# An attention and expert kernel on one core: first expert's weight splits behind its chunks, last chunks in block order, new order tables

## The chip, the cores and the metric

One core of a Trainium2 chip runs the whole program. The metric is device time in microseconds (us); lower is better. The engines are TensorE (PE in the profile; its weight loads are PEld), VectorE (DVE), ScalarE (ACT), GpSimd (POOL) and SyncE (SP), which only issues DMAs. ScalarE and GpSimd issue some DMAs of their own.

## The reference

Two layers, float32, 8 batches of 576 tokens. First an attention with landmarks (Nystrom), 8 heads of 64; then a mixture of 8 experts in which a token mostly keeps the expert of the token before it.

```python
# attention, for each batch and head; means over groups of 18 tokens give 32 landmarks
A, Bm, C = sm(q, k_lm), sm(q_lm, k_lm), sm(q_lm, k)
Z = Bm.T / (norm1(Bm) * norminf(Bm) + 1e-6)
for _ in range(6): Z = 2 * Z - Z @ Bm @ Z
x = A @ Z @ C @ v
# experts, for each token s of a batch
fresh = argmax(x[s] @ w_gate)
e = fresh if s == 0 or sigmoid(x[s] @ w_local) < 0.5 else prev_e
out[s] = softmax(x[s] @ w_gate)[e] * (relu(x[s] @ w1[e]) @ w2[e])   # w1 512x1024, w2 1024x512
```

## The kernel before, in words

**Attention.** For each batch the queries and keys come in transposed. `landmarks` (L228) sums groups of 18 tokens on VectorE, after a first halving on GpSimd (L241, L242) except for the first loads (L235, L237), and ScalarE scales them (L247, L249). `scores_c` (L262) is the matmul of landmarks against all keys (L274); `newton_step` (L427) is one step of the inverse (L432 on TensorE, L435 on VectorE), `c_v` (L335) multiplies by the values, `newton_w` (L444) leaves a small matrix `wt` for each head. The attention output is never formed: `w_w1` (L674) multiplies `wt` into the expert's w1 (L694) and splits the product into a high and a low part, `gh` (L707) and `gl` (L708), so that matmuls of the fast float32 kind keep their accuracy. The softmaxed scores are split in the same way (L516 and L520; L528 and L530 in the first batch).

**Experts.** Nearly all tokens of a batch go to one expert. `expert` (L756) runs 16 chunks for each batch: two passes over the tokens (blocks 2, 3, 4 and then 0, 1, of 128 tokens each; block 4 has 64) of 8 chunks f each. A chunk is `mm1` (L728): 6 matmuls (L737), a relu on ScalarE (L746, L748), its low part on VectorE (L749, L752); and, two chunks later (LAG = 2), `after`: three matmuls per full block (L789) and two for block 4 (L781) against chunk f of w2, which is itself split by `split_w2` (L718): ScalarE copies `raw` to `wh` (L720), GpSimd subtracts to give `wl` (L725). At the last chunk of a pass `store` (L800) scales each block and sends it out: ScalarE multiplies (L815) and issues the DMA (L816); block 4 takes L821 to L825. In the last batch block 0 is scaled on VectorE (L805) and sent from SyncE (L806), and block 1 by halves on ScalarE (L810) and VectorE (L811), sent from ScalarE (L812) and SyncE (L813). Between batches 6 and 7 a half-length expert serves up to 128 tokens that left their batch's expert.

**Order of the work.** The program is built with a scheduler: the place in the source is an instruction's priority on its engine, and the scheduler follows a simulated timeline of its own and takes the next ready instruction. The order on each engine is then fixed in the program. The source order comes from a loop over chunks (L1374 on); `events` holds the attention steps of the next batches with a time in chunks (FIRST, SECOND, PLANS, SLOT_AT), and `run` emits those that are due. G_AT, W2_AT place `w_w1` and w2 loads.

**The opening** (`first_attention`, L1013) is emitted by hand, and `line_up` (L198) fixes the order of TensorE, ScalarE, VectorE and GpSimd as emitted. `keep_warm` (L171) issues idle matmuls on zeros, SUMS[i] of them between Newton steps. The first batch's expert is not known from votes as in the others but guessed early: `guess_sums` (L532, matmuls L539), `guess_copy`, `guess_scores` (L547, 8 matmuls L551, a copy L554), `guess` (L556, VectorE L559 and L560), which puts the expert's number into `regs`. `first_weights` (L1221) then lets SyncE read it and issue the loads of w1 (two pieces, L671), of w2 chunks 0 and 1 (L715), of the keys of batch 1, of w1's second half, of w2 chunks 2 and 3 and then 4 to 7. After the opening the source has `cut_w2(0, f)` for f = 0 to 3, then the chunks; at chunk i `cuts_at` adds the split of chunk 4 + i ahead of that chunk's own matmuls. The first 9 chunks' matmuls are fixed in order by `line_up`, while attention steps that `run` emits on the whole chunk are only placed behind what was lined up.

```python
    first_attention(sts[0], sts[1])
    line_up()
    for f in range(4):
        cut_w2(0, f)
    ...
            cuts_at(b, i)      # b == 0: cut_w2(0, 4 + i)
            next(gen)          # mm1 of chunk i, with its relu
            ...
            run(t0 + i + 0.5)
            next(gen)          # after(i - 2)
```

Of the kernel before, what the change touches and what calls it, by code (L numbers as in the profile page):

```python
# [9 lines left out]
F32 = mybir.dt.float32  # L10
# [10 lines left out]
P = 128  # L21
# [55 lines left out]
def nystrom_attn_then_sticky_moe(ctx, tc, qT, kT, v, wg, w12, out):  # L77
# [678 lines left out]
    def expert(st, w2, passes, store, apart=False):  # L756

        waiting = []
        for s0, n, blocks in passes:
            yps, hs = {}, {}  # L760
            for f in range(NC2):
                hs[f] = mm1(st, f, s0, n, apart)
                yield
                if len(waiting) == LAG:
                    waiting.pop(0)()

                def after(f=f, blocks=blocks, yps=yps, hs=hs):
                    full = [k for k in blocks if k < 4]
                    for k in full:
                        if k not in yps:  # L770
                            yps[k] = py.tile([P, DM], F32, name="py")
                    wh, wl = w2[f]
                    h = hs[f][0]
                    if 4 in blocks:


                        for ff in range(0 if f == NC2 - 1 else NC2, NC2) if apart else (f,):
                            if 4 not in yps:
                                yps[4] = pg.tile([P, DM], F32, name="pg")
                            for w in w2[ff]:  # L780
                                nc.tensor.matmul(yps[4], hs[ff][1], w, start=(ff == 0 and w is w2[ff][0]),  # L781
                                                 stop=(ff == NC2 - 1 and w is w2[ff][1]))
                        if f == NC2 - 1:
                            store(4, yps[4])
                    terms = ((0, wh), (0, wl), (384, wh))
                    each = [(i, t) for i in range(len(full)) for t in terms] if f == NC2 - 1 else [
                        (i, t) for t in terms for i in range(len(full))]
                    for i, (part, w) in each:
                        nc.tensor.matmul(yps[full[i]], h[:, part + i * P:part + i * P + P], w,  # L789
                                         start=(f == 0 and part == 0 and w is wh), stop=(f == NC2 - 1 and part == 384))  # L790
                    if f == NC2 - 1:
                        for k in full:
                            store(k, yps[k])

                waiting.append(after)
                yield
        for after in waiting:
            after()

    def store(b, st, k, yp):  # L800
        ys = fk.tile([P, DM], F32, name="ys", bufs=2)
        t0 = b * S + k * P
        if b == B - 1 and k == 0:
# [209 lines left out]
    def first_attention(st, st1):  # L1013
# [288 lines left out]
    SECOND = dict(v=4.1, q0=0.1, k0=0.1, c0=0.6, q2=0.6, k2=1.1, c1=2.6, norms=2.6, a0=6.1, nf=7.1, a1=7.1, t0=7.1,
        amax=8.1, n0=7.6, t2=7.6, n1=7.6, t4=7.6, aexp=8.1, n2=7.6, cv=8.1, n3=7.6, n4=8.1, anorm=8.1, n5=8.1, nw=8.1,
        gw=8.1, aback=8.6, gates=8.6, nwt=11.1, votes=8.6, split=8.6, w1=9.1, w1b=11.2, fresh=11.6, sticky=12.1,
        chosen=14.6, own=17.6)
    STEPS = ("load v q0 k0 c0 q2 k2 c1 norms a0 nf a1 t0 n0 t2 amax n1 t4 aexp n2 cv n3 anorm n4 aback n5 "
             "nw gw gates nwt votes split w1 fresh sticky chosen own").split()
    PLANS = {
        2: (-13.4, -11.4, -9.9, -12.4, -7.9, -9.4, -7.9, -7.4, -6.9, -6.4, -6.9, -4.9, -2.4, -5.4, -1.4, -1.4, 0.1,
            -0.4, -0.9, -0.4, -0.4, 1.1, 2.6, -0.9, 4.6, 4.6, 5.1, 5.6, 7.1, 7.1, 8.1, 10.1, 8.1, 8.1, 8.6, 13.6,  # L1310
            14.1),
        3: (-22.4, -16.9, -19.4, -13.9, None, -15.4, -13.4, -13.4, -13.4, -9.9, -8.4, -8.4, -6.4, -6.9, -2.9, -7.9,
            -8.4, -6.4, -7.9, -4.4, -2.9, -3.9, -3.4, -2.4, 1.1, 2.6, 2.6, 2.6, 3.1, 5.1, 4.1, 4.1, 7.6, 5.1, 7.1,
            11.1, 11.6),
        4: (-24.4, -20.9, -18.4, -17.4, None, -16.4, -15.4, -15.4, -14.9, -14.9, -14.9, -13.4, -11.4, -11.9, -10.9,
            -8.9, -7.4, -7.4, -6.4, -8.4, -6.4, -6.4, -6.4, -7.4, -5.9, -5.4, -3.9, -3.9, 2.6, 4.1, 2.6, 2.6, 3.6,
            4.1, 5.1, 6.6, 11.6),
        5: (-26.9, -20.4, -25.4, -24.4, None, -16.9, -18.4, -16.9, -16.9, -16.4, -12.9, -14.9, -10.9, -11.4, -10.4,
            -11.9, -10.9, -10.4, -7.9, -11.4, -7.9, -9.9, -7.9, -4.4, -3.9, -1.9, -1.4, 0.6, 1.1, 4.1, 2.6, 5.6, 3.6,
            3.6, 4.1, 4.1, 6.6),  # L1320
        6: (-21.4, -17.9, -20.9, -20.4, None, -17.4, -17.9, -16.9, -13.9, -14.9, -13.9, -14.4, -11.4, -13.4, -9.9,
            -12.4, -9.9, -9.9, -5.9, -8.4, -6.9, -9.4, -5.4, -4.9, -0.9, -3.4, -2.9, -2.4, 0.6, 2.6, 1.6, 3.6, 3.1,
            3.1, 3.6, 6.6, 7.6),
        7: (-27.4, -20.4, -25.9, -19.4, None, -20.4, -20.4, -17.4, -14.9, -16.4, -14.9, -13.9, -13.4, -14.4, -11.9,
            -12.9, -11.4, -10.9, -11.9, -10.4, -9.9, -10.4, -10.4, -9.4, -5.4, -6.9, -5.9, -5.4, -0.4, -3.9, -0.4,
            1.1, 1.6, 3.6, 7.6, 7.6, 10.1),
    }
# [40 lines left out]
    first_attention(sts[0], sts[1])  # L1368
    line_up()
    others_ = (ET.Activation, ET.DVE, ET.Pool)  # L1370
    for f in range(4):
        cut_w2(0, f)
    t0 = 0
    for b in SEQ:  # L1374
# [5 lines left out]
        for i in range(LEN[b]):  # L1380
# [64 lines left out]
```

## Time and profile before

| | us |
|---|---|
| three runs | 477.02, 477.85, 478.03; median 477.85 |
| the profiled execution | 476.7 |
| its span, first to last instruction | 474.9 |
| TensorE busy in the span | 456.8 (96%), clock granted 0.994 of full on the mean |
| VectorE, GpSimd, ScalarE busy | 268.7, 231.5, 204.6 |

The profile comes from one execution. Its rows give for a group of instructions the line, the engine, the operation, output and input tiles and shapes, how long they took, and in square brackets how long the engine stood idle before and what ended that. In the table of stretches each row gives a window, its length, and the busy time of each engine with its count of instructions, then the granted TensorE clock (1.00 is 2.4 GHz, 0.50 is 1.2 GHz), the mean busy share of the DMA engines and their GB/s. A DMA row ends with the median time from issue to landing. Matmuls overlap, so that a row of six lasts less than six times one.

### The profile page before, as it was taken

How to read it: one execution, taken by the hardware profiler on the slowest of the kernel's cores; microseconds unless marked ns; L12 is line 12 of the kernel's file. 1: busy time of each engine (PE TensorE's matmuls, PEld its weight loads, DVE VectorE, ACT ScalarE, POOL GpSimd, SP SyncE). 2: the span in 40 equal slices, each digit the busy share in tenths (PEclk: the TensorE clock that was granted, in tenths of full speed). 3: DMA queues.
4: the chain of work that ended last, by engine and by line, in shares of the span. 5: the costliest groups of instructions: out<-in, count | busy, mean ns of one | idle time of the engine just before them, and what ended most of it. 6: DMA issues, size and time to landing. Idle time of an engine off the chain costs nothing.

```text
span 474.9 us, 12149 instructions
## 1 busy us (share of the span) xinstructions
PE 456.8 (96%) x4710; PEld 338.1 (71%) x4710; DVE 268.7 (57%) x824; ACT 204.6 (43%) x518; POOL 231.5 (49%) x365
## 2 busy tenths in 40 slices
PE   8979999999999999999999999999999999999995
PEld 2636667687786777768885687767886887778884
DVE  6887766776477548648633673248549834323211
ACT  2456244554164616355244634354334513555131
POOL 7178473395187508538612542144336755467010
PEclk9989999999999999999999999999999999999999
DMA  8996083964099226937842245523511731762011
GB/s 296 307 382 216 15 307 109 372 229 147 13 359 348 93 67 252 363 93 248 312 153 54 92 158 191 147 73 140 222 58 52 235 130 47 235 218 71 0 57 47
DMA packets 38861, 82.01 MB, mean 173 GB/s; under 512 B 3291, under 2 KB 4827, under 8 KB 38032
## 3 DMA queue, kind: packets, MB, share of 16 engines
q1 hardware_dynamic: 32208, 67.09, 41.2%
q10 hardware_dynamic: 5104, 9.05, 5.4%
q0 software_dynamic: 1488, 5.07, 2.8%
q8 instruction: 38, 0.62, 0.6%
q14 instruction: 23, 0.19, 0.1%
HBM read 66.29 MB, written 14.94 MB: 171 GB/s over the span
## 4 chain that ended last, share of the span: by engine, by line
PE 76%; DVE 7%; DMA 6%; issue 4%; ACT 3%; POOL 2%; SPq 1%; ACTq 0%; POOLq 0%; DVEq 0%
PE py L789 33%; PE ph L737 20%; PE pg L781 5%; DMA raw<-w 3%; PE ph L694 3%; PE one L432 2%; PE one L345 2%; DMA k_t<-kT 2%; PE one L482 2%; PE one L331 2%; DMA q_t<-qT 1%; PE one L304 1%; PE one L274 1%; DVE h L749 1%; POOL t L241 1%
## 5 line engine op out<-in xcount | busy, mean ns | idle before, releaser
L789 PE MATMUL py<-wh,h 128*128 128x512 f32 x528 | 170.4, 402 | 1.4 <-ACT ys L815 1.1
L725 POOL TENSOR_TENSOR wl<-raw,wh 128x512 fp32r<-128x512 f32 x68 | 86.9, 1294 | 73.2 <-ACT wh L720 65.0
L789 PEld LDWEIGHTS py<-wh,h 128*128 128x128 f32 x528 | 95.1, 188 | 29.2 <-issue 7.1
L746 ACT ACTIVATE h<-ph 128x256 fp32r<-128x256 f32 (+2 forms) x136 | 54.7, 403 | 128.9 <-PE ph L737 115.1
L749 DVE SCALAR_TENSOR_TENSOR h<-ph,h 128x256 fp32r<-128x256 f32 (+1 forms) x136 | 55.6, 410 | 94.0 <-ACT h L746 88.7
L789 PE MATMUL py<-wl,h 128*128 128x512 f32 x264 | 91.4, 393 | 0.0
L737 PE MATMUL ph<-ath,gh 128*128 128x320 f32 (+1 forms) x256 | 79.9, 312 | 1.9 <-DVE h L749 1.0
L737 PE MATMUL ph<-atl,gh 128*128 128x320 f32 (+1 forms) x256 | 75.8, 296 | 0.4 <-DVE atl L530 0.4
L737 PE MATMUL ph<-ath,gl 128*128 128x320 f32 (+1 forms) x256 | 75.8, 296 | 0.0
L737 PEld LDWEIGHTS ph<-ath,gh 128*128 128x128 f32 x256 | 48.1, 188 | 17.4 <-issue 6.2
L789 PEld LDWEIGHTS py<-wl,h 128*128 128x128 f32 x264 | 49.5, 188 | 10.8 <-issue 0.8
L737 PEld LDWEIGHTS ph<-atl,gh 128*128 128x128 f32 x256 | 48.1, 188 | 4.0 <-DVE atl L530 0.7
L737 PEld LDWEIGHTS ph<-ath,gl 128*128 128x128 f32 x256 | 48.2, 188 | 0.9 <-issue 0.7
L720 ACT CAST wh<-raw 128x512 fp32r<-128x512 f32 x68 | 41.0, 631 | 15.7 <-DMA raw<-w 13.9
L824 POOL TENSOR_TENSOR ys<-ys,yl 64x512 f32<-64x512 f32 x8 | 10.2, 1276 | 40.1 <-ACT yl L822 40.1
L494 POOL TENSOR_TENSOR sa<-sa,mxa 128x1152 f32<-128x1152 f32 x7 | 14.9, 2131 | 21.8 <-DVE mxa L493 21.8
L815 ACT ACTIVATE ys<-py,pall 128x512 f32<-128x512 f32 x30 | 19.9, 692 | 11.4 <-DMA out<-ys 8.3
L241 POOL TENSOR_TENSOR t<-q_t 128x288 f32<-128x288 f32 x28 | 21.4, 785 | 4.3 <-DVE sk L242 1.7
L708 DVE TENSOR_TENSOR gl<-ph,gh 128x512 fp32r<-128x512 f32 (+1 forms) x19 | 12.4, 656 | 18.7 <-ACT gh L707 18.7
L781 PE MATMUL pg<-wl,h 128*128 128x512 f32 x56 | 22.4, 400 | 0.0
L781 PE MATMUL pg<-wh,h 128*128 128x512 f32 x56 | 22.3, 399 | 0.0
L707 ACT CAST gh<-ph 128x512 fp32r<-128x512 f32 (+1 forms) x19 | 10.6, 564 | 25.2 <-PE pg L694 24.3
(338 smaller groups left out, 729.2 us busy)
## 6 DMA issues: line engine op xcount, KB each, us to landing
raw<-w SPq DMA_DIRECT2D x68, 256.0 KB, 5.3
raw<-w SPq DMA_DIRECT2D x17, 1024.0 KB, 6.9
v_t<-v SPq DMA_DIRECT2D x8, 1024.0 KB, 6.0
out<-ys ACTq DMA_DIRECT2D x30, 256.0 KB, 2.6
q_t<-qT SPq DMA_DIRECT2D x6, 1152.0 KB, 5.7
k_t<-kT SPq DMA_DIRECT2D x6, 1152.0 KB, 8.7
ad<-sa POOLq DMA_DIRECT2D x8, 576.0 KB, 3.1
q_t<-qT SPq DMA_DIRECT2D x4, 576.0 KB, 9.3
```

Of the source, the lines that this page charges most:

```text
L241: nc.gpsimd.tensor_add(t9[:, i], src[:, a + i, :, 0:9], src[:, a + i, :, 9:18])
L494: nc.gpsimd.tensor_tensor(out=sa, in0=sa, in1=mx.unsqueeze(2).broadcast_to([P, 2 * NJ, M]), op=ALU.subtract)
L694: mm = nc.tensor.matmul(ps[g][32 * c:32 * c + 32, 0:n * P], w, w1[r, n * i:n * i + n, a * P:a * P + P], start=True, stop=True)
L708: last = nc.vector.tensor_tensor(out=gl[:, g, x], in0=ps[g][:, 0:n * P], in1=gh[:, g, x].bitcast(F32), op=ALU.subtract)
L720: cut = nc.scalar.copy(out=wh, in_=raw)
L725: nc.gpsimd.tensor_tensor(out=wl, in0=raw, in1=wh.bitcast(F32), op=ALU.subtract)
L737: mm = nc.tensor.matmul(hp, w[:, g, c], x[:, g, s0:s0 + n], start=(i == 0), stop=(i == 5))
L746: nc.scalar.activation(out=h[:, 0:e], in_=hp[:, 0:e], func=AF.Relu)
L749: nc.vector.scalar_tensor_tensor(out=h[:, 384:384 + m], in0=hp[:, 0:m], scalar=0.0, in1=h[:, 0:m].bitcast(F32), op0=ALU.max, op1=ALU.subtract)
L781: nc.tensor.matmul(yps[4], hs[ff][1], w, start=(ff == 0 and w is w2[ff][0]), stop=(ff == NC2 - 1 and w is w2[ff][1]))
L789: nc.tensor.matmul(yps[full[i]], h[:, part + i * P:part + i * P + P], w, start=(f == 0 and part == 0 and w is wh), stop=(f == NC2 - 1 and ...
L815: nc.scalar.mul(out=ys, in_=yp, mul=st["pw"][:, k:k + 1])
```

## The change

Six edits. (1) In `first_attention` the matmuls that guess the expert go ahead of two idle matmuls, and the VectorE part of the guess goes ahead of the second half of the score maxima, `c_exp(1)` and Newton step 1; SUMS[0] goes from 2 to 1. (2) Only w2 splits 0 and 1 are emitted ahead of the first chunk; split 2 + i is emitted behind `mm1` of chunk i. (3) In the last chunk of every pass the matmuls on w2 are chained in the order written: three for one block, then three for the next. (4) In the last batch block 0 is scaled on ScalarE as other blocks are, block 1 on VectorE in one piece, and both are sent from ScalarE's queue. (5) SECOND, FIRST, PLANS, G_AT, SLOT_AT, W2_AT have new numbers. (6) `cuts_at` no longer splits for batch 0.

```diff
                     terms = ((0, wh), (0, wl), (384, wh))
                     each = [(i, t) for i in range(len(full)) for t in terms] if f == NC2 - 1 else [
                         (i, t) for t in terms for i in range(len(full))]
+                    mms = []
                     for i, (part, w) in each:
-                        nc.tensor.matmul(yps[full[i]], ...)
+                        mms.append(nc.tensor.matmul(yps[full[i]], ...))
+                    if f == NC2 - 1:
+                        in_row(mms)
...
-        if b == B - 1 and k == 0:
+        if b == B - 1 and k == 1:
             nc.vector.tensor_scalar(out=ys, in0=yp, scalar1=st["pw"][:, k:k + 1], scalar2=None, op0=ALU.mult)
-            nc.sync.dma_start(out=out[t0:t0 + P, :], in_=ys)
-        elif b == B - 1 and k == 1:
-            yr = fk.tile([P, 256], F32, name="yl", bufs=1)
-            nc.scalar.mul(out=ys[:, 0:256], in_=yp[:, 0:256], mul=st["pw"][:, k:k + 1])
-            nc.vector.tensor_scalar(out=yr, in0=yp[:, 256:512], scalar1=st["pw"][:, k:k + 1], scalar2=None, op0=ALU.mult)
-            nc.scalar.dma_start(out=out[t0:t0 + P, 0:256], in_=ys[:, 0:256])
-            nc.sync.dma_start(out=out[t0:t0 + P, 256:512], in_=yr)
+            nc.scalar.dma_start(out=out[t0:t0 + P, :], in_=ys)
         elif k < 4:
             nc.scalar.mul(out=ys, in_=yp, mul=st["pw"][:, k:k + 1])
             nc.scalar.dma_start(out=out[t0:t0 + P, :], in_=ys)
...
-        SUMS = (2, 2, 2, 2)
+        SUMS = (1, 2, 2, 2)
...
         newton_step(0, st, 0)
         idle = psa.tile([P, 512], F32, name="one")
+        guess_scores(st)
         keep_warm(SUMS[1], idle)
-        guess_scores(st)
+        guess(st)
         c_max(1, 1)
         c_exp(1)
         newton_step(0, st, 1)
-        guess(st)
         keep_warm(SUMS[2], idle)
...
     def cuts_at(b, i):
-        if i < 5:
+        if b and i < 5:
             cut_w2(b, NC2 - 5 + i)
-        if b == 0 and i < 4:
-            cut_w2(b, NC2 - 4 + i)
...
-    SECOND = dict(v=4.1, q0=0.1, k0=0.1, c0=0.6, q2=0.6, k2=1.1, c1=2.6, ..., split=8.6, w1=9.1, w1b=11.2, fresh=11.6, ...
+    SECOND = dict(v=3.6, q0=0.1, k0=0.6, c0=0.6, q2=0.1, k2=1.1, c1=1.6, ..., split=10.1, w1=8.6, w1b=9.7, fresh=10.1, ...
-    FIRST = dict(rs=0.6, rm=0.6, re=0.6, rn=1.1, rb=2.1, gw=3.1, gates=3.6, votes=5.6, fresh=6.1, ...
+    FIRST = dict(rs=0.1, rm=0.1, re=0.1, rn=1.6, rb=2.6, gw=1.6, gates=3.6, votes=5.1, fresh=5.6, ...
-    W2_AT = (11, 12, 12, 12, 12, 15)
+    W2_AT = (10, 12, 12, 13, 15, 15)
...
-    for f in range(4):
+    for f in range(2):
         cut_w2(0, f)
...
             cuts_at(b, i)
             next(gen)
+            if b == 0 and i < NC2 - 2:
+                cut_w2(b, 2 + i)
             if t0 + i < IN_ROW:
                 line_up((ET.PE,), others_ if i < 4 else ())
```

In PLANS (batches 2 to 7, 37 steps each) 70 entries move earlier, 68 later, and the rest stay; most by half a chunk or one, the farthest by 3.5 chunks (`split` of batch 2, later) and 3 (`w1` of batch 7, later). G_AT of batch 4 goes from chunks (11, 14) to (10, 13); SLOT_AT moves by 0.5 to 2.5 chunks.

## Rows read from the trace of the kernel before

**Rows 1.** The page's head: span, and busy time of TensorE and its weight loads.
```profile
span 474.9 us, 12149 instructions
PE 456.8 (96%) x4710; PEld 338.1 (71%) x4710; DVE 268.7 (57%) x824; ACT 204.6 (43%) x518; POOL 231.5 (49%) x365
```

**Rows 2.** Table of stretches: window, length, busy us by engine, clock, DMA share, GB/s.
```profile
30.00:32.70 2.70, 0.17 (x2) 0.00 (x0) 2.09 (x5) 1.79 (x6) 1.41 (x2) 1.00 1.08 394
32.70:36.10 3.40, 3.36 (x32) 0.93 (x32) 2.54 (x9) 1.74 (x7) 3.40 (x5) 0.50 1.00 407
36.10:42.00 5.90, 5.90 (x46) 4.00 (x44) 3.48 (x8) 4.87 (x16) 5.90 (x6) 1.00 0.35 129
42.00:54.00 12.00, 10.92 (x83) 8.30 (x79) 11.14 (x45) 5.11 (x20) 8.32 (x17) 1.00 0.45 147
54.00:469.20 415.20, 409.52 (x4149) 311.50 (x4149) 225.33 (x695) 179.31 (x434) 197.02 (x275) 1.00 0.47 162
469.20:474.90 5.70, 0.00 (x0) 0.00 (x0) 1.01 (x2) 0.47 (x1) 0.00 (x0) 0.84 0.27 95
```

**Rows 3.** The chain of waits, 20 to 33 us: start, us, what.
```profile
23.23 8.27 DMA raw<-w
```

**Rows 4.** Timeline, 27 to 33 us, ScalarE, VectorE and TensorE: start, length, instruction.
```profile
27.02 1.15 ACT L720 CAST wh<-raw 128x512 fp32r<-128x512 f32 x2
28.02 0.74 DVE L242 TENSOR_REDUCE sq<-t 128x64 f32<-128x576 f32 x1
...
30.85 1.29 ACT L720 CAST wh<-raw 128x512 fp32r<-128x512 f32 x2 [2.68 <-DMA raw<-w]
...
32.05 0.38 ACT L746 ACTIVATE h<-ph 128x256 fp32r<-128x256 f32 x1
...
32.43 0.26 ACT L247 ACTIVATE ql<-sq 128x64 f32<-128x64 f32 x1
...
32.74 1.94 PE L274 MATMUL one<-k_t,ql 64*32 64x288 f32 x12 [2.57 <-ACT ql L247]
```

**Rows 5.** Timeline, 16 to 19 us: the guess of the expert and the Newton update beside it.
```profile
16.27 0.60 PE L176 MATMUL one<-zeros 128*128 128x512 bf16 x2
...
16.71 0.45 DVE L1052 TENSOR_REDUCE mx<-ph 128x1 f32<-128x288 f32 x1
...
17.10 0.17 ACT L554 COPY tot<-one 128x8 f32<-128x8 f32 x1 [0.91 <-PE one L551]
...
17.55 0.29 DVE L435 TENSOR_TENSOR et<-ph,et 128x128 f32<-128x128 f32 x1 [0.20 <-PE ph L432]
...
18.03 0.16 DVE L560 FIND_INDEX8 regs<-top,tot 128x8 uint32<-128x8 f32 x1
...
18.93 0.99 SPq L671 DMA_DIRECT2D raw<-w  x2
```

**Rows 6.** TensorE's waits over the whole span: us in total, times, longest.
```profile
PE py L789 <- ACT ys L815: 1.1, 2, 0.6
```

**Rows 7.** Timeline of the tail: last matmuls, VectorE's scaling, SyncE's last store.
```profile
468.56 0.61 PE L789 MATMUL py<-wh,h 128*128 128x512 f32 x2
469.05 0.75 DVE L805 TENSOR_SCALAR ys<-py,pall 128x512 f32<-128x512 f32 x1 [2.18 <-PE py L789]
...
470.28 0.37 SPq L813 DMA_DIRECT2D out<-yl  x1
```

**Rows 8.** DMA issues by line: count, KB each, median us to landing.
```profile
raw<-w SPq DMA_DIRECT2D x68, 256.0 KB, 5.3
...
out<-ys ACTq DMA_DIRECT2D x30, 256.0 KB, 2.6
...
out<-yl SPq DMA_DIRECT2D x1, 128.0 KB, 2.6
```

**Rows 9.** VectorE's L520 by length (min/median/max ns), and the wait behind the longest.
```profile
L520 DVE TENSOR_TENSOR atl<-at,ath x7: 1324/1357/2737, 82.3 to 378.2; 128x1152 fp32r<-128x1152 f32 x7
...
190.33 0.39 PE L737 MATMUL ph<-ath,gh 128*128 128x256 f32 x1 [0.99 <-DVE h L749]
```

More of the change, by code (lines that the diff above doesn't have):

```diff
@@ L787, in after @@
                         (i, t) for t in terms for i in range(len(full))]
+                    mms = []
                     for i, (part, w) in each:
-                        nc.tensor.matmul(yps[full[i]], h[:, part + i * P:part + i * P + P], w,
-                                         start=(f == 0 and part == 0 and w is wh), stop=(f == NC2 - 1 and part == 384))
+                        mms.append(nc.tensor.matmul(yps[full[i]], h[:, part + i * P:part + i * P + P], w,
+                                                    start=(f == 0 and part == 0 and w is wh), stop=(f == NC2 - 1 and part == 384)))
+                    if f == NC2 - 1:
+                        in_row(mms)
                     if f == NC2 - 1:
@@ L1300, in at_time @@
         events.append((t, len(events), fn))
[L1302 to L1305, printed above, removed]
+    SECOND = dict(v=3.6, q0=0.1, k0=0.6, c0=0.6, q2=0.1, k2=1.1, c1=1.6, norms=2.6, a0=6.1, nf=7.1, a1=7.1, t0=7.6,
+        amax=7.6, n0=7.6, t2=7.6, n1=7.6, t4=7.6, aexp=8.1, n2=7.6, cv=7.6, n3=7.6, n4=8.1, anorm=8.6, n5=8.1, nw=8.1,
+        gw=8.1, aback=8.6, gates=8.6, nwt=12.1, votes=8.6, split=10.1, w1=8.6, w1b=9.7, fresh=10.1, sticky=10.1,
+        chosen=14.1, own=20.1)
     STEPS = ("load v q0 k0 c0 q2 k2 c1 norms a0 nf a1 t0 n0 t2 amax n1 t4 aexp n2 cv n3 anorm n4 aback n5 "
@@ L1308, in nystrom_attn_then_sticky_moe @@
     PLANS = {
[L1309 to L1326, printed above, removed]
-    }
@@ L1328, in nystrom_attn_then_sticky_moe @@
-    G_AT = {0: (14, 15), 1: (14, 15), 2: (13, 15), 3: (14, 15), 4: (11, 14), 5: (13, 15), 6: (13, 14), 7: (2, 7)}
-    SLOT_AT = (-13.5, -4.5, -8.0, -4.0, -2.0, 0.5, 1.5, 9.0, 8.6, -0.5, 26.5)
+        2: (-13.9, -11.4, -10.4, -13.4, -7.9, -9.4, -7.9, -7.4, -7.4, -6.4, -7.4, -4.4, -2.4, -4.9, -1.4, -1.4, 0.6,
+            -0.4, -1.4, -0.4, 0.1, 0.1, 1.6, -2.4, 6.6, 5.1, 5.1, 6.1, 6.6, 6.6, 8.1, 13.6, 8.1, 8.1, 9.1, 13.6,
+            14.6),
+        3: (-22.4, -16.9, -20.9, -13.9, None, -14.4, -14.4, -13.4, -13.4, -9.9, -8.4, -8.9, -6.4, -7.9, -3.4, -7.9,
+            -8.4, -6.4, -7.9, -3.4, -2.9, -3.9, -2.4, -2.4, 1.1, 1.6, 1.6, 1.6, 3.6, 4.1, 3.6, 4.6, 8.6, 4.6, 6.1,
+            12.1, 12.6),
@@ new lines, in nystrom_attn_then_sticky_moe @@
+        4: (-25.4, -20.9, -19.4, -18.9, None, -16.9, -16.9, -15.9, -15.4, -15.4, -14.9, -14.4, -11.9, -12.4, -10.4,
+            -7.9, -8.4, -7.9, -5.9, -8.4, -6.4, -5.9, -4.9, -6.9, -4.9, -5.4, -5.4, -3.9, 2.6, 4.1, 2.6, 2.6, 4.6,
+            3.1, 5.1, 6.1, 12.1),
+        5: (-26.9, -22.4, -26.4, -24.9, None, -16.9, -16.9, -16.9, -16.9, -16.9, -12.9, -15.9, -10.9, -11.4, -10.4,
+            -12.9, -11.4, -10.9, -7.9, -10.4, -7.9, -10.4, -7.4, -4.9, -4.4, -1.9, -0.9, 0.6, 1.1, 3.1, 2.1, 5.1, 3.6,
+            3.6, 4.6, 5.6, 7.1),
@@ new lines, in nystrom_attn_then_sticky_moe @@
+        6: (-21.9, -18.4, -20.9, -20.9, None, -16.9, -17.9, -15.4, -15.4, -14.4, -12.4, -13.9, -9.9, -11.9, -8.9,
+            -12.4, -10.4, -9.9, -5.9, -8.9, -6.9, -8.9, -4.9, -4.9, -0.9, -4.4, -3.9, -2.9, -0.9, 0.6, 1.6, 3.1, 3.6,
+            3.1, 4.1, 7.6, 7.6),
+        7: (-25.9, -18.9, -25.4, -18.4, None, -19.9, -20.9, -17.4, -17.4, -14.9, -14.9, -13.4, -13.4, -14.4, -11.9,
+            -11.9, -10.9, -10.4, -11.9, -10.4, -9.4, -9.9, -9.4, -9.4, -4.9, -6.9, -5.4, -5.4, -0.9, -3.4, 0.1, 1.6,
+            4.6, 2.6, 7.1, 8.1, 10.6),
+    }
@@ L1330, in nystrom_attn_then_sticky_moe @@
+    G_AT = {0: (14, 15), 1: (14, 15), 2: (13, 15), 3: (14, 15), 4: (10, 13), 5: (13, 15), 6: (13, 14), 7: (2, 7)}
+    SLOT_AT = (-15.0, -3.0, -7.0, -4.0, -2.5, 3.0, 1.5, 8.0, 6.6, -1.5, 26.0)
     TURN = 6
-    FIRST = dict(rs=0.6, rm=0.6, re=0.6, rn=1.1, rb=2.1, gw=3.1, gates=3.6, votes=5.6, fresh=6.1, sticky=6.1,
-        chosen=6.1, own=7.1)
-    W2_AT = (11, 12, 12, 12, 12, 15)
+    FIRST = dict(rs=0.1, rm=0.1, re=0.1, rn=1.6, rb=2.6, gw=1.6, gates=3.6, votes=5.1, fresh=5.6, sticky=6.1,
+        chosen=6.1, own=7.6)
```

## The prediction

> **What bounds the kernel now.** I read the page first: TensorE is busy for 456.8 of 474.9 us [rows 1], so what is to be had is its 18.1 us of idle time and any stretch at a lower clock. The table of stretches says where these lie [rows 2]: 2.53 us idle in 30.0 to 32.7; 1.08 in 42 to 54; 5.68 spread over 54 to 469.2 (1.4% of that stretch); 5.70 behind the last matmul. The rest, some 3 us, lies before 30 us. One stretch is special: in 32.7 to 36.1 TensorE works all the time, but at a granted clock of 0.50, that is 1.2 GHz. It had stood idle for 2.57 us just before. The 3.36 us of work there would take half as long at 2.4 GHz, so the clock costs 1.7 us and the pair 4.2 us.
>
> The chain of waits names the cause: 8.27 us of a w2 load [rows 3]. The timeline shows how a load stops TensorE [rows 4]. ScalarE copies w2 chunks 0 and 1 and is done at 28.17; its next instruction is the copy of chunk 2, whose load lands only at 30.85, and behind that stand the copy of chunk 3 (to 32.14), the relu of the first expert chunk (32.05) and `ql`, the scaling of batch 1's queries (32.43). `ql`'s input was there at 28.76, and it lets TensorE go on at 32.74. The relus and `ql` need none of these copies. This is an order on ScalarE's queue, not ScalarE's load.
>
> From 36 us on TensorE is full and the other engines are hidden behind it, save where one of them is dense for a while: VectorE for 11.14 of the 12 us of 42 to 54 [rows 2]. So microseconds saved in the opening stay saved only as far as VectorE keeps up.
>
> **The change, part by part.** The sum is made against the profiled execution, 476.7 us (span 474.9), which is 1.15 below the median of the three runs, 477.85; the sum is carried over to that median.
>
> *Guess earlier.* The eight guess matmuls no longer stand behind two idle ones (0.60 us), so the copy L554 starts up to 0.6 us before 17.10; I take 0.4. VectorE's guess then follows it instead of the Newton update that started at 17.55. The expert's number, now there at 18.19, comes at about 17.35, and the loads issued at 18.93 [rows 5] go out about 0.8 us earlier. The DMA engines are full in 30 to 36 [rows 2], so I let the queue as a whole shift: chunk 2 lands at about 30.05 instead of 30.85. No SyncE instruction is added; the reading of the register and the loads behind it only move up.
>
> *What it delays.* VectorE now has the guess (some 0.45 us) and the score maximum (0.45, the row at 16.71) ahead of Newton step 1's update at 17.55 [rows 5]. That step and all behind it come about 0.4 us later; the one idle matmul less before gives 0.1 back. The first expert chunk starts +0.3 us.
>
> *Splits behind chunks.* Chunk 2's copy now has a lower priority than the first relu, chunk 3's than the second. If ScalarE takes the relu first, `ql` comes at about 29.7 and TensorE, through with its second chunk at 30.17 + 0.3, has no wait. If the scheduler still finds the copy ready first, one copy (0.6 us) instead of two stands behind the load, and TensorE starts at about 30.05 + 0.6 + 0.85 (relu and `ql`, 31.6 at the latest). I take 31.0, as the simulated timeline decides and either is open: 1.7 us before 32.74. The idle time is then 0.5 us. TensorE kept its full clock over the 0.99 us wait at 189 to 190 ([rows 9]; the clock is 1.00 throughout the long stretch of [rows 2]), so the 1.7 us of half clock go too: -3.4 us in all, bounds 0 and -4.2. What is late next is VectorE: TensorE meets the dense stretch of 42 to 54 earlier. VectorE's idle time in 30 to 42 is 0.6 + 0.9 + 2.4 us [rows 2]; some of it is waiting for the same stall and closes, the rest cannot be called up at will. I give back 0.8 us, bounds 0 (the idle time takes all) and 2.0 (only the 1.4 us idle in 30 to 36 are recovered). GpSimd's subtractions come later in the source, but chunk f is used at chunk f + 2 and each is hidden behind 2 chunks of TensorE work. Opening: **-2.6 us**.
>
> *Last chunks in block order.* The six matmuls of a block pair take the same time in any order, so this is worth only what an earlier store gives. TensorE waited twice, 1.1 us in all, until ScalarE had emptied a block's bank at a pass change [rows 6]. Now the first block ends one matmul ahead of the second; with the chain it ends three ahead, and its store can start some 0.45 us earlier (two overlapping matmuls take 0.61 [rows 7]). I take -0.5, bounds 0 and -1.1. A chain makes TensorE wait where the low part is late; VectorE makes it two chunks before, which hides it.
>
> *The tail.* Today block 1's right half waits for VectorE's 0.75 us on block 0, and its DMA goes out last, at 470.28 [rows 7]. Then block 0 is finished some 0.5 us earlier and goes through ScalarE and its queue while TensorE finishes; block 1's 0.75 us on VectorE start at the end of the last matmul, 469.17 plus some 0.08, and its DMA is issued at about 470.06: -0.2 us. The store is then 256 KB instead of 128; landing took 2.6 us for both [rows 8], so I add nothing. Bounds -0.4 and +0.3 (ScalarE's queue holds block 1's store while it issues block 0's, one issue of 0.37).
> The Trainium skill ("DMA: Bandwidth & Descriptors", "Anatomy of one DMA") gives a transfer a fixed part of about 2.0 us plus its bytes at 436 GB/s; by that the larger last store would land 0.3 us later (an estimate from that page) and the tail would come out at +0.1 instead. The two medians of the trace do not show it.
>
> *New tables.* As many of the 222 entries of the later batches move later as earlier, mostly by half a chunk. W2_AT's later loads are hidden behind batch 0's second pass; without that cover a batch would wait one landing, 5.3 us [rows 8]. The trace cannot price the sum. From below: all of the 5.68 us idle in 54 to 469.2 less the 1.1 already counted, -4.6. From above: one wait of 0.99 us as at 190 [rows 9] in five more batches, +5. I take 0, nearest to the row that shows this stretch 98.6% full already, and put 1.5 either way into the range.
>
> Sum: -2.6 - 0.5 - 0.2 + 0 = -3.3; 476.7 becomes 473.4, and the median 477.85 becomes **474.5 us**.
>
> **The rivals.** (a) *The copy stays in front and the clock still falls.* For it: the scheduler takes what its timeline finds ready, and it put chunks 2 and 3 ahead of the relu before. TensorE starts at 31.5 instead of 32.74, no clock is regained, 0.8 is given back: -0.4, and with -0.7 from the ends 476.7. Against: the idle time would be 1 us, which at 190 left the clock alone. Chance 0.15.
> (b) *VectorE becomes the bound* in 42 to 54: only the 1.4 us it stood idle in 30 to 36 are regained; -1.4 - 0.7 gives 475.8. For it: 93% busy there, and TensorE waits 1.08 us already; against: c1's and q2's VectorE work also moves up in the source. Chance 0.15.
> (c) *Slower: the tables move softmax splits beside GpSimd.* L520 takes 1.32 to 1.36 us, but 2.74 once, with GpSimd at work beside it; the relu's low part stood behind it and TensorE waited 0.99 [rows 9]. One of seven pays now. With five more paying, +5.0 - 3.3 gives 479.5; from four more on the gain is gone. Against: the moves have both signs. Chance 0.15.
> The Trainium skill ("SBUF — State Buffer", "Who interferes with whom") says that a VectorE instruction with both inputs in SBUF shuts out, or waits for, a GpSimd one that reads SBUF; L520 is of that form, and the long one agrees.
> (d) *The order on ScalarE does not change*, two copies still first; only the loads' 0.8 us less the 0.3 of delay is gained: 477.3. Chance 0.10.
>
> **How the numbers follow.** Forecast 0.45, the rivals 0.15, 0.15, 0.15, 0.10. A difference of 0.2%, 0.96 us, is what a measurement of this kernel can tell, so faster means below 476.9. Nearly all of the forecast, most of (b), over half of (a) and a part of (d) lie there: 0.66. Within 0.2%: the rest of (a) and (d) and edges, 0.19. Slower: most of (c), and a lost tail together with (d): 0.15. The range goes down to 472.2 (no wait at 31 us, nothing given back, -4.2 + 0.3, and 1.7 from tables, turns and tail), and up to 478.7, which takes in (a), (b), (d) and the nearer part of (c).
>
> **What would show it.** Right: ScalarE has the first relu ahead of the third w2 copy; no TensorE wait over 1 us at L274; no window at 0.50 clock near 33 us; SyncE's w1 loads before 18.3; the first L737 later by 0.2 to 0.4; ScalarE's last store issued near 470.0 less the gain. Wrong: a new TensorE wait over 1 us in 30 to 54 on VectorE's L749, GpSimd's L725 waited for by L789, or more than 7 us of idle time behind 54.

## The result and the profile after

| | before | after | ratio, 95% interval |
|---|---|---|---|
| first comparison, 4 runs each | 477.44 (476.67 to 478.03) | 472.98 (472.64 to 473.50) | 0.9917 [0.9888, 0.9946] |
| a later one, 32 and 12 runs | 475.78 (474.20 to 477.10) | 473.79 (473.21 to 475.26) | 0.9968 [0.9956, 0.9981] |

The change makes the kernel faster, by 4.5 us in the first comparison and by 2.0 in the second. The forecast of -3.3 lies between the two. The profiled execution took 473.5 us, the highest of its four, against 476.7 before.

The page's head, to be read against [rows 1]:

```profile
span 471.8 us, 12124 instructions
PE 455.4 (97%) x4705; PEld 337.8 (72%) x4709; DVE 270.0 (57%) x823; ACT 204.6 (43%) x518; POOL 234.8 (50%) x365
```

The table of stretches of the kernel after, with the windows of [rows 2] up to 54 us, then to its last matmul and its end:

```profile
30.00:32.70 2.70, 2.07 (x43) 0.74 (x48) 2.70 (x9) 1.03 (x6) 2.70 (x4) 1.00 1.07 412
32.70:36.10 3.40, 3.40 (x32) 2.49 (x17) 3.21 (x9) 2.19 (x6) 2.22 (x3) 1.00 1.00 390
36.10:42.00 5.90, 5.29 (x35) 3.13 (x33) 3.61 (x11) 2.88 (x13) 4.48 (x5) 1.00 0.07 26
42.00:54.00 12.00, 10.14 (x75) 7.10 (x75) 10.41 (x42) 5.58 (x21) 9.40 (x20) 1.00 0.43 147
54.00:465.80 411.80, 408.05 (x4130) 311.02 (x4128) 225.42 (x691) 180.22 (x435) 200.05 (x272) 1.00 0.48 163
465.80:471.80 6.00, 0.00 (x0) 0.00 (x0) 0.74 (x1) 0.00 (x1) 0.00 (x0) 0.77 0.24 89
```

The stretch at 0.50 is gone: -1.7 us. The idle time at 30 us fell from 2.53 to 0.63, but 42 to 54 went from 1.08 to 1.86, 36 to 42 from 0 to 0.61, and 22 to 30 from 0.97 to 1.49: from 22 to 54 us TensorE stands idle 4.59 us where it stood 4.62. The stall came back in pieces, and over them the clock stayed at 1.00. Behind 54 us the idle time ahead of the last matmul fell from 5.7 to 3.7, and the tail grew by 0.3. So the profile's 3.2 us are, to about 0.2, the clock (1.7) and the long stretch (2.0), less the tail (0.3).

Part of the 3.2 is not the change's. The second half of batch 0's queries arrived sooner in this execution: VectorE's second `sq`, which sums them, began 0.73 us earlier. The timeline of VectorE, before and then after:

```profile
8.32 1.35 DVE L237 TENSOR_REDUCE sq<-q_t 128x64 f32<-128x1152 f32 x1 [1.01 <-DMA q_t<-qT]
```
```profile
7.59 1.35 DVE L237 TENSOR_REDUCE sq<-q_t 128x64 f32<-128x1152 f32 x1
...
16.28 0.16 DVE L560 FIND_INDEX8 regs<-top,tot 128x8 uint32<-128x8 f32 x1
```

From that instruction to the end of the span the kernel before takes 466.6 us and the change 464.2, in a second profile of it 464.6: 2.0 to 2.4 us less, near the second comparison.

The timeline of the opening, ScalarE and then TensorE, answers to [rows 4]:

```profile
26.53 1.17 ACT L720 CAST wh<-raw 128x512 fp32r<-128x512 f32 x2
28.40 1.30 ACT L720 CAST wh<-raw 128x512 fp32r<-128x512 f32 x2 [0.70 <-DMA raw<-w]
29.60 0.38 ACT L746 ACTIVATE h<-ph 128x256 fp32r<-128x256 f32 x1
...
29.98 0.26 ACT L247 ACTIVATE ql<-sq 128x64 f32<-128x64 f32 x1
...
30.29 0.69 PE L274 MATMUL one<-k_t,ql 64*32 64x288 f32 x8 [0.60 <-ACT ql L247]
```

ScalarE still takes copies 2 and 3 ahead of the first relu; only copies 4 to 7 moved. The wait shrank because the loads landed 2.45 us earlier (28.40 for 30.85). FIND_INDEX8, which ends the guess, ended at 16.44 for 18.19; of these 1.75 us 0.73 is the earlier start. Measured from the second `sq` the guess ends 9.87 to 9.89 us later in six profiles with the old place and 8.82 to 9.10 later in eight with the new one. So of the 2.45 us 0.73 is the start and 1.0 the guess. The last 0.7 goes with SyncE's queue: its two issues of the loads of chunks 0 and 1 (L715) took 0.88 us in all eight and 1.60 to 2.49 in the six. What held them there is open. SyncE's timeline, before and then after:

```profile
20.11 1.80 SPq L715 DMA_DIRECT2D raw<-w  x2
```
```profile
18.36 0.88 SPq L715 DMA_DIRECT2D raw<-w  x2
```

### The profile page after: what moved, and what is told of

It is laid out like the page before. It is cut to its first block, busy times and chain, and to the rows that moved or that the text cites. A ratio compares the mean times of both kernels' runs of the same rounds, so it can differ in the third digit from the quotient of the medians.

```text
span 471.8 us, 12124 instructions
## 1 busy us (share of the span) xinstructions
PE 455.4 (97%) x4705; PEld 337.8 (72%) x4709; DVE 270.0 (57%) x823; ACT 204.6 (43%) x518; POOL 234.8 (50%) x365
## 4 chain that ended last, share of the span: by engine, by line
PE 76%; DVE 8%; DMA 6%; ACT 4%; issue 3%; POOL 2%; SPq 0%; POOLq 0%; ACTq 0%; DVEq 0%
PE py L790 34%; PE ph L737 20%; PE pg L781 5%; DMA raw<-w 3%; DMA k_t<-kT 3%; PE ph L694 3%; PE one L432 2%; PE one L345 2%; PE one L482 2%; PE one L304 1%; PE one L331 1%; POOL t L241 1%; DVE h L749 1%; ACT ec L317 1%; DVE sq L242 1%
## 5 line engine op out<-in xcount | busy, mean ns | idle before, releaser
L749 DVE SCALAR_TENSOR_TENSOR h<-ph,h 128x256 fp32r<-128x256 f32 (+1 forms) x136 | 55.4, 409 | 83.0 <-ACT h L746 78.3
L737 PE MATMUL ph<-ath,gh 128*128 128x320 f32 (+1 forms) x256 | 79.8, 312 | 2.3 <-DVE h L749 1.4
L737 PE MATMUL ph<-atl,gh 128*128 128x320 f32 (+1 forms) x256 | 75.9, 297 | 0.4 <-DVE atl L530 0.4
L737 PE MATMUL ph<-ath,gl 128*128 128x320 f32 (+1 forms) x256 | 76.0, 297 | 0.0
L737 PEld LDWEIGHTS ph<-ath,gh 128*128 128x128 f32 x256 | 48.1, 188 | 19.8 <-issue 6.1
L737 PEld LDWEIGHTS ph<-atl,gh 128*128 128x128 f32 x256 | 48.1, 188 | 4.2 <-DVE atl L530 0.7
L737 PEld LDWEIGHTS ph<-ath,gl 128*128 128x128 f32 x256 | 48.1, 188 | 0.5 <-issue 0.3
L781 PE MATMUL pg<-wl,h 128*128 128x512 f32 x56 | 22.4, 400 | 0.0
L241 POOL TENSOR_TENSOR t<-k_t 128x288 f32<-128x288 f32 x24 | 19.6, 840 | 5.5 <-DMA k_t<-kT 1.4
L241 POOL TENSOR_TENSOR t<-q_t 128x288 f32<-128x288 f32 x28 | 20.4, 747 | 3.7 <-DVE sk L242 1.3
L781 PE MATMUL pg<-wh,h 128*128 128x512 f32 x56 | 22.2, 397 | 0.0
```

The lines of the kernel that those rows point to most:

```text
L241: nc.gpsimd.tensor_add(t9[:, i], src[:, a + i, :, 0:9], src[:, a + i, :, 9:18])
L737: mm = nc.tensor.matmul(hp, w[:, g, c], x[:, g, s0:s0 + n], start=(i == 0), stop=(i == 5))
L749: nc.vector.scalar_tensor_tensor(out=h[:, 384:384 + m], in0=hp[:, 0:m], scalar=0.0, in1=h[:, 0:m].bitcast(F32), op0=ALU.max, op1=ALU.subtract)
```

## The experiments

Theory 1, 2 and 3 in the texts below are: the earlier loads do it; the splits' place does it, as predicted; the parts work only together. In the later texts P stands for parts that need one another (from 3), Q for parts that each add their own (from 2), and R for a layout that any edit changes by chance.

**One part on the kernel before.** The edits are the change's own hunks, one at a time.

```diff
# guess: edit (1)
-        SUMS = (2, 2, 2, 2)
+        SUMS = (1, 2, 2, 2)
...
# splits: edits (2) and (6)
-    for f in range(4):
+    for f in range(2):
...
# ends: edits (3) and (4)
+                    if f == NC2 - 1:
+                        in_row(mms)
...
# tables: edit (5)
-    SECOND = dict(v=4.1, q0=0.1, k0=0.1, ...
+    SECOND = dict(v=3.6, q0=0.1, k0=0.6, ...
...
```

Guess: 

> The kernel before with the earlier guess alone (the guess right behind its scores, one idle matmul less ahead of it). Theory 1, from the two traces: the loads that the guess releases land earlier, so ScalarE's copy of chunk 2 waits under 1 us instead of 2.68, TensorE's 2.57 us of idle time at 30 us shrinks below 1.3, and the 0.50 clock behind it goes; 1.4 to 2.5 us faster than before, nearly all of the clock and none of the idle time. Theory 2, as I predicted it: the loads come 0.8 us earlier, the copies still stand in front and the clock still falls; 0.4 to 0.8 us faster, a stretch at 0.50 behind a wait of some 1.8 us. Theory 3, the parts fit one another only as a whole: no gain, or slower, as TensorE's later idle time grows by what the opening gives.

Splits: 

> The kernel before with the later w2 splits behind the chunks in the source, alone. Theory 1: copies 2 and 3 stay ahead of the first relu on ScalarE's queue as they do with the whole change; the wait for the load stays near 2.6 us and the 0.50 clock stays; within 0.5 us of before. Theory 2, as I predicted it: the first relu goes ahead of copy 2, the wait goes from 2.57 to about 0.5 and the half clock with it; 1.5 to 3.4 us faster. Theory 3: within 0.5 us or slower.

Ends: 

> The kernel before with the last chunks in block order and the last two blocks each whole on ScalarE's queue, alone. Theory 1 and theory 2 alike: the two waits for ScalarE at a pass change, 1.1 us in all, fall to about 0.6; the last store is issued 0.2 to 0.3 us sooner after the last matmul but lands later by as much; 0.3 to 0.9 us faster. Theory 3: as the schedule of the whole run is laid out anew by any edit, anything within 2 us either way, with TensorE's idle time in 54 us to the last matmul anywhere from 4 to 8.

Tables: 

> The kernel before with the new tables alone. Theory 1: the tables carry most of the 2.0 us by which TensorE's idle time behind 54 us fell; 1 to 2 us faster, idle time there under 4.7. Theory 2, as I predicted it: 0, within 0.5 us. Theory 3: the tables were fitted to a run whose opening is 3 us earlier; in the old opening they do nothing or harm, 0 to 2 us slower.

| alone on before (477.54, 29 runs) | median | ratio, 95% interval |
|---|---|---|
| guess | 482.22 | 1.0093 [1.0066, 1.0120] |
| splits | 477.83 | 1.0012 [0.9991, 1.0032] |
| ends | 477.96 | 1.0005 [0.9985, 1.0026] |
| tables | 475.64 | 0.9967 [0.9944, 0.9989] |

The four differences add up to +3.5 us, where the whole gives -2.0 to -4.5: theory 3. The splits alone leave copies 2 and 3 ahead of the relu and TensorE waits 2.4 us at L274, as theory 1 has it; theory 2's step is refuted. The ends alone bring no gain: TensorE waits for ScalarE at a pass change three times (1.7 us), not twice. (The profiled execution was the second longest of its twelve, 480.1 us; the load of chunk 2 landed late in it, and the wait at L274 was 4.4 us.) The tables alone give 1.9 us, in theory 1's range; the idle time behind 54 us, 4.8, missed its bound by 0.1.

The guess alone mends the clock of the opening (1.00 all through 30 to 36 us, behind a wait of 1.8 us at L274, where theory 1 had under 1.3) and loses it later. The table of stretches of this run, 66 to 78 us, and its timeline on ScalarE, VectorE and TensorE:

```profile
66.00:72.00 6.00, 2.89 (x33) 2.58 (x31) 3.75 (x7) 0.79 (x3) 5.50 (x7) 0.82 0.67 235
72.00:78.00 6.00, 5.69 (x58) 3.36 (x58) 2.04 (x6) 1.95 (x10) 0.84 (x2) 0.61 0.20 74
```
```profile
67.82 0.37 ACT L746 ACTIVATE h<-ph 128x256 fp32r<-128x256 f32 x1
...
68.95 1.38 DVE L512 STREAM_TRANSPOSE at<-sa 128x1152 f32<-128x1152 f32 x1 [0.81 <-POOL sa L505]
...
70.26 0.39 DVE L749 SCALAR_TENSOR_TENSOR h<-ph,h 128x256 fp32r<-128x256 f32 x1
...
70.70 0.58 PE L737 MATMUL ph<-ath,gh 128*128 128x256 f32 x1 [2.17 <-DVE h L749]
```

L749, the low part of a relu, had its input at 68.19. VectorE stood at L512, which waited for GpSimd; TensorE stood idle 2.17 us and then worked at a granted clock of 0.50 until 76.4 us (0.61 on the mean of 72 to 78). The scheduler had laid the transpose ahead of L749. In the kernel before the two stand the other way round at this place. It is the fault of the opening over again, on another engine.

**The change without one part.** The same hunks, taken back one at a time.

Without guess: 

> The changed kernel with the guess put back where it was. Theory P (guess and tables need each other): near the tables alone, 474.5 to 476.5 us, with the 2.3 to 2.6 us wait at L274 and the 0.50 clock behind it back. Theory Q (each part adds its own, as I predicted): 0.8 us slower than the changed kernel, about 473.8, as the splits keep the wait small. Theory R (any edit lays the schedule out anew, and what comes is chance): a new idle time of over 1.5 us at a place where neither kernel has one.

Without splits: 

> The changed kernel with the first expert's later splits put back in front of the chunks in the source. Theory P: copies 4 and 5 come between the first relu and ql, as in the run with the guess alone, 1.2 us more of waiting at L274 (1.8 instead of 0.6), the clock stays; 473.5 to 474.8 us. Theory Q: the relus stand behind the copies again and the half clock is back; 1.7 to 3.4 us slower than the changed kernel, 474.7 to 476.4. Theory R: a new idle time of over 1.5 us somewhere behind 42 us.

Without tables: 

> The changed kernel with the old tables. Theory P: the old tables set behind the earlier opening the same wrong order as in the run with the guess alone (VectorE's transpose L512, which waits for GpSimd's L505, ahead of the second pass of a relu, L749): over 2 us of idle time at 66 to 72 us and a clock under 0.9 behind it; 4 to 8 us slower than the changed kernel, 477 to 481. Theory Q: no difference, 472.5 to 473.5. Theory R: slower, with its idle time at another place than 66 to 72.

Without ends: 

> The changed kernel without the block order of the last chunks and with the old stores. Theory P and theory Q: 0 to 0.7 us slower than the changed kernel, two waits of 0.5 to 0.6 us for ScalarE at the pass changes instead of one. Theory R: 1 to 3 us slower, with a new idle time of over 1.5 us at a place that has nothing to do with the last chunks.

| change without (before 477.20, 23 runs) | median | ratio to before, 95% interval |
|---|---|---|
| guess | 476.53 | 0.9990 [0.9973, 1.0006] |
| splits | 474.08 | 0.9935 [0.9913, 0.9957] |
| tables | 479.27 | 1.0043 [1.0023, 1.0062] |
| ends | 474.03 | 0.9932 [0.9909, 0.9954] |

The whole change, which was not measured beside these four, stands at 0.9917 and 0.9968 in its two comparisons, so that splits and ends can't be told from nothing by their times, while the tables carry 0.75 to 1.26% (3.6 to 6 us) and the guess 0.2 to 0.7%. The guess gains with the new tables and loses 4.7 us without them; the tables give 1.9 us alone and two to three times that with the guess: theory P, as far as the times go. Guess and tables were not run together without the other two parts.

Theory P's mechanisms held by half. Without the guess the wait at L274 is back with 1.8 us, for the 2.3 to 2.6 expected, in the fastest of its twelve executions (474.5 us), and the clock falls behind it. Without the splits copy 4 does stand ahead of the first relu and copy 5 ahead of `ql`, 1.2 us of copies, and the wait at L274 is 1.9 us; but the clock fell as well (0.69 on the mean of 32.7 to 36.1), which P did not expect. So the splits' new place, idle by itself, keeps these two copies out of the way once the loads come earlier. Without the ends two waits of 1.1 us in all are back.

Without the tables I had expected L512 ahead of L749 again. The time came as P had it, the place as R had it: not 66 to 72 us but 48 to 54. VectorE and TensorE there, and the stretches around it:

```profile
49.28 0.79 DVE L653 TENSOR_SCALAR psum<-psum 128x5 f32<-128x5 f32 x1
49.98 0.76 DVE L403 TENSOR_TENSOR nrc<-s 128x2 f32<-128x2 f32 x1
...
51.22 0.21 DVE L752 SCALAR_TENSOR_TENSOR hx<-ph,hx 128x64 fp32r<-128x64 f32 x1
...
51.57 0.47 PE L781 MATMUL pg<-wh,hx 128*128 128x512 f32 x1 [1.43 <-DVE nrc L405]
```
```profile
48.00:54.00 6.00, 4.21 (x30) 2.42 (x33) 5.41 (x22) 1.38 (x6) 3.61 (x9) 0.99 0.55 183
54.00:60.00 6.00, 6.00 (x65) 4.02 (x50) 2.72 (x12) 0.52 (x3) 1.08 (x6) 0.72 0.05 17
```

Two tiny VectorE instructions last 0.79 and 0.76 us beside GpSimd's two sums L241 (49.30 to 50.72) and end with them. In the kernel after they take 0.24 and 0.15: L403 is through at 49.09 and the sums begin at 49.10. L781 needs `hx` (L752), which stands behind both on VectorE; the profile names L405, the instruction next to it. TensorE waits 1.43 us, and the clock is 0.72 on the mean of 54 to 60 us. The Trainium skill ("SBUF — State Buffer", "Who interferes with whom") says that VectorE and GpSimd can shut each other out of the SBUF ports that they share for a whole instruction; the trace agrees, at about 0.6 us for each of the two.

**The change once more, and three orders.** All four were measured together, on one chip (before: 475.78, 32 runs).

```diff
# b5_forced (kernel before with the splits) and a6_forced (kernel after)
         cut = nc.scalar.copy(out=wh, in_=raw)
+        not_ahead_of(cut, mark)    # copy 2: ql of batch 1; copy 3: the second relu
...
             run(t0 + i + 0.5)
+            if b == 0 and i < NC2 - 2:
+                cut_w2(b, 2 + i)
# a5_oldfirst (kernel after)
-    SECOND, FIRST = new numbers
+    SECOND, FIRST = old numbers
```

Change again: 

> The changed kernel once more, in the same call as the next three. All theories: 472.3 to 473.8 us; from the last matmul to the end of the span 5.6 to 6.1 us, as in the five profiles with the new stores so far, against 5.7 with the old ones.

Order forced on before: 

> The kernel before with the later splits, and with copy 2 bound behind the first relu and ql, copy 3 behind the second relu, on ScalarE's queue: the order that I predicted and that the change did not bring. Guess and tables are the old ones, and the loads land as late as before. Theory Q (my step): the wait of 2.4 us at L274 falls to 0.5 or less, the clock stays at 1.00, and 2.6 us are gained: 474.4 to 475.5. Theory P (an opening that is earlier is worth nothing under the old tables): the wait and the half clock go, but the idle time from 36 us on grows by as much or more, with a wait of over 1 us or a clock under 0.9 in 42 to 78 us: 476.5 to 480. A third way: TensorE waits for copy 2 itself at the first matmul that uses it, 1 us or more before 42 us, and little is gained.

Old tables of batches 0 and 1: 

> The changed kernel with the old tables for batches 0 and 1 alone (FIRST and SECOND); the tables of batches 2 to 7, the slot's and the w2 loads' are the new ones. Theory P1 (the two early tables hold the opening's gain, as VectorE is dense in 42 to 54): idle time there over 2.4 us and a clock under 0.9 in 48 to 66 us, as with all tables old; idle time behind 120 us under 3.5 as with all tables new; 476 to 479 us. Theory P2 (the later tables hold it): 472.5 to 474 us, no such wait.

Order forced on after: 

> The changed kernel with copies 2 and 3 bound behind the first relu and ql, and behind the second relu. Theory Q: the 0.6 us wait at L274 goes to 0.2 or less, GpSimd's sums for batch 1's queries come ahead of two subtractions and the 0.6 us idle time at 40 us goes too; 471.5 to 472.6 us. Theory P: as the tables fit the opening as it was, a wait of over 1 us comes up in 42 to 78 us; 473.5 to 477.

| | median | ratio to before, 95% interval |
|---|---|---|
| change again | 473.79 | 0.9968 [0.9956, 0.9981] |
| order forced on before | 477.13 | 1.0019 [1.0002, 1.0036] |
| change with old FIRST, SECOND | 479.79 | 1.0077 [1.0046, 1.0107] |
| order forced on after | 474.86 | 0.9984 [0.9969, 1.0000] |

Forced on the kernel before, the order came out as I had predicted it, and did not help. ScalarE's timeline of that run (its lines are shifted: L749 is the relu, L722 the copy, L251 the scaling of batch 1's keys), and TensorE's wait:

```profile
28.69 0.38 ACT L749 ACTIVATE h<-ph 128x256 fp32r<-128x256 f32 x1 [0.36 <-PE ph L740]
...
29.07 0.26 ACT L247 ACTIVATE ql<-sq 128x64 f32<-128x64 f32 x1
32.23 0.62 ACT L722 CAST wh<-raw 128x512 fp32r<-128x512 f32 x1 [2.90 <-DMA raw<-w]
32.76 0.25 ACT L251 ACTIVATE k_t<-sk 128x64 f32<-128x64 f32 x1
```
```profile
33.06 0.47 PE L276 MATMUL one<-k_t,ql 64*32 64x320 f32 x4 [2.12 <-ACT k_t L251]
```

The relu and `ql` are free at 29.3; the next instruction behind the late copy, the keys' scaling, now holds TensorE for 2.12 us, and the clock is 0.50 in 34 to 36 us. The time lies in P's range, but not for P's reason. It is the third way of that expectation in another dress: the wait was handed on to the next in the queue. Holding the copy behind the keys too was not tried.

Forced on the kernel after, the 0.6 us at L274 go, 1.0 and 1.1 us of waits for VectorE come (`sa`, and at 45 us the transpose L1114), and the clock in 45 to 48 us is 0.60 on the mean: 1.1 us slower than the change measured beside it, as P had it (the profiled execution, 476.4 us, is one of the longer of its twelve; the median is 474.9).

With the two early tables alone put back the loss is 6.0 us against the change measured beside it, no smaller than with all tables old. P2 is refuted; P1 is not shown. The idle time in 42 to 54 us is 2.38 (P1: over 2.4), the clock 0.96 there and 0.79 in 54 to 60, but the time is 0.8 us above P1's range and its bound for the time behind 120 us failed widely: 6.5 us of idle time, where the change has 2.8. So over half of the loss (3.7 of 6.4 us between the two profiles) lies where the tables are the new ones. Old early and new later tables seem not to fit each other, and that the early ones alone hold the gain is not shown. One wait of 2.14 us stands there. ScalarE, then TensorE:

```profile
150.56 0.62 ACT L720 CAST wh<-raw 128x512 fp32r<-128x512 f32 x1 [3.79 <-DMA raw<-w]
151.67 0.62 ACT L720 CAST wh<-raw 128x512 fp32r<-128x512 f32 x1 [0.49 <-DMA raw<-w]
152.19 0.38 ACT L746 ACTIVATE h<-ph 128x256 fp32r<-128x256 f32 x1
```
```profile
153.08 0.39 PE L737 MATMUL ph<-ath,gh 128*128 128x256 f32 x1 [2.14 <-DVE h L749]
```

A relu behind copies whose loads are late: what [rows 4] shows at 30 us, 120 us later. No other run has a median below the change's 473.79, but the change without splits (0.9935) and without ends (0.9932) has a lower ratio than the whole in its second comparison (0.9968): that these two parts bring anything is not shown.

## Why the prediction was right, and where it was not

The total held by luck in part: two errors offset each other.

*Guess earlier: right, its loads mis-sized.* I took 0.84 us for the guess; with the arrival of the queries taken off it is 1.0 in the profile after. I let chunk 2's load shift by the same 0.8, and from the same start it landed 1.7 us earlier.

*What it delays: right in size here, not in kind.* The first L737 starts 18.57 us behind the second `sq` instead of 18.32: +0.25, where I had +0.3. But VectorE's later Newton step delays nothing: the first matmul of L694, behind the Newton steps, starts 15.61 us behind `sq` for 15.57. TensorE then stops at L694 itself, behind its first matmul. The timeline after, and the waits of the change's second profile:

```profile
24.08 0.45 PE L694 MATMUL ph<-raw,wt 64*32 64x256 f32 x8 [0.48 <-issue]
```
```profile
PE ph L694 <- issue: 1.3, 1, 1.3
```

No trace shows what it waits for. In that second profile the first L737 comes 19.32 us behind `sq`: +1.0. Over the eight profiles with the new guess it is 18.35 to 19.51, over the six with the old one 18.31 to 18.33.

*Splits behind chunks: the step that failed.* I read the place in the source as the order on ScalarE, with the other way out left open (as rival (d), 0.10, for the time). In no profile with the change's own splits does the relu stand ahead of copy 2. The 1.7 us of half clock were saved all the same, as the earlier loads cut the idle time to 0.6; without the earlier guess, with the splits in their new place, the wait is 1.8 us and the clock falls. And the relu's order would not have been enough: forced, it hands the wait to the keys' scaling, of which I had not asked what stands behind the copy after `ql`. Rival (d) was right on the order and wrong on the worth of the loads, which I had as 0.8 us and no clock.

*Give-back: right in kind, short in size.* I took 0.8 us in 42 to 54; it is 0.78 there, and 1.1 more in 22 to 30 and 36 to 42.

*Block order: right in the whole* (one wait of 0.6 us instead of two, for my -0.5), *not alone* (three, 1.7 us). It takes the new early tables: with the block order and the old FIRST and SECOND there are three waits as well (1.3 and 1.5 us).

*Tail: wrong by 0.3 us.* I had -0.2, and it grew by 0.1. The last rows of the kernel after answer to [rows 7]:

```profile
465.37 0.39 PE L790 MATMUL py<-wh,h 128*128 128x512 f32 x1
465.79 0.75 DVE L808 TENSOR_SCALAR ys<-py,pall 128x512 f32<-128x512 f32 x1 [2.34 <-PE py L790]
...
466.58 0.34 ACTq L809 DMA_DIRECT2D out<-ys  x1
```

The last store is issued 0.82 us behind the last matmul for 1.11 before: -0.3, where I had -0.2. But from that issue to the end of the span it is 5.03 us on the mean of eight profiles with the new store (4.83 to 5.22) and 4.60 in six with the old one (4.57 to 4.64): +0.43 where I had added nothing, as two medians of 2.6 us over all stores [rows 8] seemed to say that size costs nothing. On these means the tail is 5.85 instead of 5.71. The store's size, its queue (ScalarE's for SyncE's) and the store ahead of it on that queue changed together, so that the 0.43 is not shown to be the size alone. The Trainium skill's figure ("DMA: Bandwidth & Descriptors", "Anatomy of one DMA") gave +0.3 and a tail of +0.1, an estimate; it came nearer than mine, but that section gives the figure for DMAs that GpSimd issues, and this one is ScalarE's.

*Tables 0: the second step that failed.* Alone they give -1.9 us. With the earlier opening they are worth 3.6 to 6: without them the microseconds won before 36 us are lost, and more. I had priced them on the kernel before and by the count of their moves. One part of their worth needs no earlier opening: TensorE's idle time behind 120 us. From 120 us to the last matmul, the kernel before, the change without tables, the change, and the change without guess:

```profile
120.00:469.17 349.17, 345.10 (x3304) 264.68 (x3302) 180.99 (x557) 149.22 (x350) 160.07 (x220) 1.00 0.45 152
```
```profile
120.00:471.96 351.96, 347.18 (x3314) 266.52 (x3312) 182.74 (x560) 150.19 (x351) 160.48 (x222) 1.00 0.44 151
```
```profile
120.00:465.76 345.76, 342.98 (x3264) 263.34 (x3264) 180.23 (x553) 149.78 (x350) 163.64 (x220) 1.00 0.46 154
```
```profile
120.00:466.88 346.88, 344.31 (x3300) 264.11 (x3298) 180.39 (x554) 149.79 (x350) 163.32 (x220) 1.00 0.45 153
```

That is 4.07, 4.78, 2.78 and 2.57 us idle; over all profiles 3.6 to 5.4 in six with the old tables and 2.6 to 3.3 in seven with the new ones. The rest lies ahead of 120 us, where with the earlier guess the old tables bring the waits at 50 and 70 us and the half clock. I read it so that the new tables lay the engines' orders for an opening that ends some 2 us earlier; this is argued, as no run had tables other than the old, the new and one mix of them. The forecast "VectorE is late next, 0.8 us" and rival (b) had the place of the danger (42 to 54), not that the tables decide it.

*Slips in the sums.* The latest start of TensorE is 31.6 us in one place and 31.5 in rival (a); the terms add up to 31.5. VectorE's idle time in 30 to 36 us is 1.5 us, not 1.4. Rival (d) leaves out the 0.7 us that (a) and (b) take for ends and tail; with these it stands at 476.6.

*What would show it.* Right: SyncE's w1 loads at 17.17, no 0.50 window, no wait over 1 us at L274. Wrong: the relu's place; and the first L737 came earlier in the span (26.16 for 26.64), as the queries did.

Open: why the gain is 4.5 us in one comparison and 2.0 in another, where the kernel before itself runs at 475.8 instead of 477.4. Measured from the second `sq` the profiles give 2.0 to 2.4, so that the moment at which the first queries land may be part of the 4.5; for the other runs no trace shows it. Over the runs of the second comparison the mean granted clock is 0.9970 with the change and 0.9946 before; by an estimate 0.0024 of 475 us is 1.1 of the 2.0, so that the clock is again over half of it. How long the wait at 30 us was in these runs of before no profile shows.

## What to carry to other kernels

In a program laid out by a scheduler the parts of a change need not add up: try each part alone and the whole without it, for the part that is slower alone (here +4.7 us) may be half of the gain, and a part that gives little alone (the tables, 1.9 us) the other half. On a queue in order, an instruction that waits for a load holds all behind it: bring the load forward, since here moving two instructions past it handed the wait to the third. Price a step by the order that comes out on the engine, not by its place in the source.

## What the runs showed of the hardware

The start scatters: VectorE's second `sq`, which waits for queries, began between 7.48 and 8.90 us in fourteen profiles of nearly the same opening, and what follows shifts with it. Two profiles of the same kernel, the change, differ by 1.3 us there and by 1.7 in their spans.

The length of a wait alone does not tell whether the clock falls. At L274 (L276 where the lines are shifted) it stayed at 1.00 behind waits of 0.6 to 1.8 us in seven profiles and fell to 0.50 behind 1.8 to 4.4 us in the other seven (1.79 us with the guess alone, where it stayed, and 1.84 without the guess, where it fell, lie close together). Elsewhere it fell to 0.50 with a wait of 2.17 us at 70 us (the guess alone) and stayed at 1.00 behind one of 2.14 us at 153 us (the old early tables). And it fell to 0.50 near waits of 1.1 to 1.4 us in three runs (the order forced on the change, the old early tables, the change without tables), with other waits shortly ahead or behind. The means given above, such as 0.60, 0.69 or 0.72, are of stretches that hold both levels.
